# A gated mix of two spectral filters on one core: l = 512 from the gate's products, and the first inverse step in column tiles

## Chip, core and metric

The kernel runs on one core of a Trainium2 chip. The metric is the device time of one execution in microseconds (us). Before the change the median of three runs is 132.49 us (131.15, 132.49 and 135.37). One further execution was recorded by the profiler. It took 130.99 us, and its instructions span 129.2 us.

## The reference

One input of 2048 x 1024 goes through two spectral filters; a gate made from each row of the input mixes the two results.

```python
def _A_ref(x, w_r, w_i):          # _B_ref is the same with B's weights
    B, S, D = x.shape
    X = jnp.fft.rfft2(x.astype(jnp.float32), axes=(-2, -1))
    X = X * (w_r + 1j * w_i)
    return jnp.fft.irfft2(X, s=(S, D), axes=(-2, -1)).astype(jnp.bfloat16)

x = A_x                            # (1, 2048, 1024), bf16
g = _sigmoid((x * gate_w).sum(-1, keepdims=True))
a = _A_ref(x, A_w_r, A_w_i)
b = _B_ref(x, B_w_r, B_w_i)
return g * a + (1 - g) * b
```

The transform has 513 columns, l = 0 to 512. Column l = 512 doesn't fit the 512 wide tiles and is carried separately.

## The kernel before

**Stages.** Everything is a matrix product with constant matrices. Row s of the input is split as 16 p + n2, with p on the 128 partitions.

1. *S1* (`xrows`, `stage_s1`): for each of 16 n2, VectorE folds the columns by symmetry and TensorE transforms over p. The result Z is kept in `R3`.
2. *gate rows* (`gate_row`, c = 0 to 3): products of Z with the folded gate weights, in column tiles of TensorE: 4 tiles of 32 output partitions work side by side, in two waves of 512 columns. An eviction (`zrow`) and four small products (`zg`) follow.
3. *D* and *S2*, for 16 groups kg: `stage_d` makes the transform along the columns (8 matmuls of 256 columns), evicted to Q; `stage_s2` finishes the transform along the rows (4 matmuls of 512 columns), evicted to X. `stage_d` also has two matmuls of one column each (into `xd`), which make column l = 512.
4. *Products* (`prod(b, m)`): for branch b (0 is A, 1 is B) and pair m of groups, 2 multiplications (2048 elements a partition) and 2 additions (1024) on VectorE. Three pairs differ. Those in `SPLIT` have the two multiplications alone, and the one in `LATE` has four of half the size; for these three the additions are left to TensorE, which accumulates four products where it otherwise takes two.
5. *First inverse step, I1* (`stage_i1`): for each kg of a pair, 4 matmuls of 128 x 128 weights and 512 columns (8 for `SPLIT` and `LATE`), then an eviction V into a tile `ub` of the ring (at most 6 at once).
6. *Turn*: from `ub` two DMAs, one for each half h of the rows, move 128 KB each from 64 partitions, 2 apart, to 8 partitions, 4 apart. They land in `U`: `R1` for A, and `R3` for B once Z has been read. There are 64 turns, all on SP's queue.
7. *Column 512* (`x512`, `p512`, `v512`): the same steps in small. It ends in two tiny writes a branch (`U5`).
8. *Second inverse step, Sj* (`inverse`): for each of 16 n2, 8 products with A's U and 8 with B's, with the gate mixed into the matrices `RA` and `RB`. Then eviction T, the inverse along the columns (`Dinv`), eviction, and four additions that unfold the result (`h0`, `h1`, `y0`, `y1`), and the output DMA. Half h = 0 of U serves n2 = 0 to 7 and h = 1 the others. An Sj of n2 = 0 to 7 needs the h = 0 turns of *all* groups of its branch.

**What sets the order.** A list scheduler (`Plan.run`) goes through all operations; `TABLE` gives each its engine (p TensorE, a ScalarE, v VectorE, s SP) and a place in that engine's queue. An operation starts in the plan when its inputs are there and its tiles are free. The engines then run the planned order in strict sequence with semaphores. SP's queue is strictly in order too: a turn that waits for its V holds up all later ones. The evictions are shared between ScalarE and VectorE as the table says.

**Lines.** L502 is every matmul, L505 every two-input VectorE operation, L529 and L530 the evictions on ScalarE and VectorE, L535 every DMA, L895 the gate's sigmoids. `RING` holds product tiles, `ub`, Q and `gz`; `SK` holds the matrices of S2 and I1; `MS` small constants; `PS` is PSUM.

Of the kernel before, what the change touches and what calls it, by code (L numbers as in the profile page):

```python
# [9 lines left out]
ALU = mybir.AluOpType  # L10
AP = bass.AP
BF = dt.bfloat16

NS = 513
# [4 lines left out]
s1374 s1438 s1501 s1564 s1627 s1690 s1754 s1817 s1880 s1944 v90 p160 v508 v522 v890 a638 p1558 a1678 v583 v441 v475  # L19
v549 p684 a830 p597 a738 v638 v698 p859 a1013 p772 a921 v829 v769 p946 a1104 p1034 a1196 v966 v1026 p1208 v1348  # L20
p1121 a1287 v1157 v1097 p1582 a1690 p1296 a1404 v1288 v1228 p1383 a1495 p1470 a1587 v1556 v1462 p1810 a1930 p1669
a1781 v1616 v1683 v1650 v1522 v1731 v1804 p1909 v1974 p1953 a2021 p1756 a1873 p1998 p2064 v2149 p2278 p2010 v2088
p2392 p2130 a2390 p2495 v2528 p2686 a2799 s1999 s2062 s2188 s2252 s2378 s2441 s2505 s2568 s2631 s2694 s2758 s2821
s2884 s2947 s3011 s3074 p2174 a2299 p2408 a2531 p2299 a2439 p2600 a2707 v2918 v3145 v3031 v3205 p3322 a3441 s3550
s3611 p3588 a3715 s3825 s3885 p2507 v2621 p2783 a2890 p2689 v2804 p2962 a3075 v3265 v3492 v3379 v3552 p4120 a4264
s4434 s4374 p3674 a3807 s3946 s4006 p2869 a2983 p3142 a3258 p3049 a3166 p3408 a3532 v3726 v3900 v3960 v4187 p4379
a4539 s4738 s4678 p4292 a4447 s4557 s4617 p3228 a3349 p3940 a4081 p3494 a3624 p3760 a3898 v4427 v4715 v4313 v4540
p4828 a4945 s5055 s5115 p5000 a5128 s5238 s5298 p3847 a3990 p4206 a4356 p4026 a4173 p4558 a4666 v4788 v5015 v4902
v5076 p5353 a5494 s5664 s5604 p5180 a5311 s5481 s5421 p4465 v4601 p4741 a4854 p4648 a4762 p5439 a5586 v5831 v6058
v5944 v6118 p6252 a6417 s6526 s6587 p6338 a6508 s6647 s6708 p5087 a5220 p5619 a5769 p5525 a5677 p5798 a5952 v6178  # L30
v6429 v6303 v6489 p6759 a6883 s7053 s6992 p6618 a6741 s6851 s6911 p5705 a5860 p6526 a6650 p5885 a6051 p6163 a6325
v6957 v7144 p7282 a7476 s7658 s7597 p7455 a7649 s7819 s7758 a6043 p6151 v6292 v7131 v6416 v7665 v8662 v8367 v8076
v8705 v8202 v4074 v4247 v3613 v3840 p5266 a5403 s5542 s6115 p4914 a5037 s5176 s6054 v7258 v7431 v7552 v7789 p7887
a7994 s8257 s8136 p7973 a8086 s8317 s8196 v5249 v5423 v5136 v5363 p6937 a7066 s7234 s7537 p6851 a6974 s7113 s7174
v5597 v5770 v5483 v5710 p6064 a6234 s6433 s6373 p5978 a6142 s6312 s6252 v6610 v6837 v6723 v6897 p7023 a7157 s7355
s7295 p7110 a7249 s7476 s7416 v7963 v8212 v8089 v8273 p8491 a8598 s8710 s8892 p8405 v8514 s8650 s8831 v7675 v7849
p8059 a8253 s8378 s8438 p8232 a8480 s8589 s8771 v7071 v7492 v7371 v6550 p7196 p7757 p7628 a7827 a7778 s7954 s7894
p7671 p7800 p7844 a7876 a7925 s8015 s8075 p8685 a8728 p8763 v8808 v8816 p8728 v8772 p8807 v9006 v9231 s5999 p6492
a6600 v8380 v8447 p6424 a6833 v8333 v8413 p6469 a8430 v8672 v8719 p6447 a8380 v8480 v8628 p8876 p9096 p9156 a9202
p9664 a9776 p8921 p9006 p9090 v9117 p9352 v9461 v9885 v9946 v10019 v10140 s10214 p8831 p9045 a9111 p9220 a9329 p9484  # L40
p9574 v9709 p9841 a9949 v10080 v10200 v10374 v10549 s10622 p9308 p9529 v9595 p10062 a10223 p10189 p10329 a10394
p10506 a10614 v10850 v10729 v11024 v11145 s11218 p9796 p9973 a10040 p10373 a10486 p9928 p10018 a10132 p10241 v10435
v10669 v10609 v10790 v11084 s11158 p9751 p10150 p10234 v10260 p10772 v10910 p10461 p10593 p10677 a10705 p10904
a11017 v11205 v11265 v11446 v11569 s11643 p10682 p10859 a10925 p11079 a11200 p10632 p10727 a10797 p10992 a11108
v11325 v11386 v11509 v11630 s11703 p9440 p9619 a9685 p11345 a11505 p11166 p11256 a11322 p11433 a11596 v11766 v11705
v11859 v11953 s12027 p11211 p11301 a11413 p11565 a11688 v11920 v11826 v12014 v12068 s12115 p11520 p11652 a11779
p11888 a11953 v12047 v12121 p11932 a12002 v12101 v12142 v12176 s12223 v12209 s12258"""
QD = False
SPLIT = ((0, 7), (1, 6))
LATE = ((1, 7),)  # L50
# [7 lines left out]
def bf16_bits(a):  # L58
    a = np.ascontiguousarray(np.asarray(a, dtype=np.float32))
    u = a.view(np.uint32).astype(np.uint64)  # L60
    return ((u + 0x7FFF + ((u >> 16) & 1)) >> 16).astype(np.uint16)


def make_consts():
# [20 lines left out]
    turned = np.array([8 * (4 * a + b) + e for a in range(4) for e in range(8) for b in range(4)])  # L85
# [62 lines left out]
    KI = KI.reshape(2, 2, 128, 2, 2, 8, 8).transpose(2, 0, 1, 3, 6, 5, 4).reshape(128, 1024)  # L148
# [4 lines left out]
    M = np.zeros((128, 410))  # L153
    for h in range(2):
        M[:, 408 + h] = (-1.0) ** (np.arange(128) + 1)
    M[turned, 280 + np.arange(128)] = 1.0
    M[:, :16] = gs.reshape(128, 1)
    M[::32, 16] = 1.0
    for kg in range(16):
        M[kg, 152 + 32 * (kg // 4) + kg % 4] = 1.0  # L160
# [292 lines left out]
def bass_gated_mix__spectral_gfnet__spectral_gfnet__prompt_kernel(  # L453
# [11 lines left out]
    def ap(t, off, dims, p0=0, np_=128):  # L465
# [10 lines left out]
    MS = sb("MS", 410)  # L476
# [70 lines left out]
    def cload(eng, t, off, key, a, b, keys, **kw):  # L547
# [3 lines left out]
    P.add("zero8", {"dve": (0.1, 0.2)}, lambda e: [lambda e: e.memset(ap(G8, 0, [[1, 8]]), 0.0)], [], ["G8"])  # L551
    P.add("table", {"act": (1.4, 1.5)}, lambda e: [lambda e: e.activation(ap(ZG, 0, [[1, 8]]), ap(G8, 0, [[1, 8]]), ACT.Sigmoid)],
          ["G8"], ["ZG"])
# [11 lines left out]
    cload("sp", MS, 0, "MS", 0, 410, ["MS"])  # L565
# [54 lines left out]
    ev("g8", 8, lambda: (ap(G8, 0, [[1, 8]]), psl(gp, 0, [[1, 8]])), [(gp,)], ["G8"], only="act")  # L620
# [4 lines left out]
    def gate_row(c):  # L625
# [3 lines left out]
        def fns():  # L629
            return [mm(psl(t, 0, [[1, 512]], 32 * j, 32), ap(G8, 2 * j + r, [[0, 32]]),  # L630
                       ap(R3, (2 * j + r) * 128 + c * 32, [[1024, 16], [1, 32]]), r == 0, r == 1)
                    for r in range(2) for j in range(4)]
        pe("gate", [512] * 2, fns, ["G8"] + [("Z", 4 * c + i, j) for i in range(4) for j in range(2)], [(t,)], alloc=[t])
        ev("zrow", 512, lambda: (rg(gz, 0, [[8, 16], [128, 4], [1, 8]]), psl(t, 0, [[32, 16], [8, 4], [1, 8]])),
# [3 lines left out]
           [(gz, 0, 1), "MS"], [(gzps,)], alloc=[gzps] if c == 0 else [])  # L638

# [69 lines left out]
    x5, xd = Tile("p1", 1), Tile("p1", 1)  # L709

    def stage_d(kg):
# [14 lines left out]
        pe("D", [256] * 8 + [1] * 2, fns, allz(kg // 8) + ["DM", "MS"], [(t,), (xd,)], alloc=[t] + ([xd] if kg == 0 else []))  # L726
# [23 lines left out]
    def prod(b, m):  # L750
# [6 lines left out]
        if (b, m) in LATE:  # L757
            p = PT[b, m] = [[Tile("tl", 2) for _ in range(2)] for _ in range(2)]
            for kg in range(2 * m, 2 * m + 2):
                P.key = ("PA", "PB")[b], m  # L760
                for c, t in enumerate(p[kg % 2]):
                    P.add("mul", vt(1024), lambda e, t=t, c=c, kg=kg: [tt(
                        rg(t, 0, [[512, 2], [1, 512]]), ap(R4, kg * 1024, [[512, 2], [1, 512]]),
                        ap(T, kg * NS + c * NW, [[NW - 2 * c * NW, 2], [1, 512]]), ALU.mult)],
                        [("X", kg)] + wkeys(b, (kg,)), [(t, 0, 2)], alloc=[t])
            return
# [15 lines left out]
    def stage_i1(b, m):  # L782
# [3 lines left out]
        wide = isinstance(p, list)  # L786
        terms = [(768, 0, 0), (1792, 0, 512), (1024, 1, 0), (1024, 1, 512)] if wide else [(768, 0, 0), (1024, 0, 512)]

        def data(r, i):
            return rg(p[terms[i][1]] if wide else p, r * 1024 + terms[i][2], [[1, 512]])  # L790

        def matrix(r, i, o, w):
            return ap(SK, terms[i][0] + (512 if r == m == 0 else 0) + o, [[1, w]])

        def turns(u, kg, parts=1):
            for h in range(2):
                def turn(h=h):
# [222 lines left out]
```

## Time and profile before

| | us |
|---|---|
| runs, lowest / median / highest | 131.15 / 132.49 / 135.37 |
| profiled execution: time, span | 130.99, 129.2 |
| busy: PE, VectorE (DVE), ScalarE (ACT) | 114.4, 106.5, 99.7 |
| TensorE clock granted, mean | 0.992 |

How to read the views: a table of windows gives, for each stretch of the span, each engine's busy time with the number of instructions, the granted clock, the share of time for which the core's 16 DMA engines were busy, and what they moved. The chain of waits follows the last instruction back to what released it. A timeline lists runs of like instructions, with start and length. Matmul ends are modelled: a 512 column matmul is shown as 379 ns, while in an unbroken stream the next one starts 0.216 us after it, so throughput is read from starts.

From the span's start: S1 and the gate rows run to about 23 us, D, S2, products, I1 and turns from there to about 94 us, and the second inverse step with its output to the end.

### The profile page before, as it was taken

The numbers are of one execution on the slowest core, as the hardware profiler recorded it, in microseconds if no ns is written. First come the engines' busy times: TensorE is split into PE (matmuls) and PEld (weight loads), VectorE is DVE, ScalarE is ACT, GpSimd is POOL, SyncE is SP. The second block draws the span as 40 slices with busy tenths as digits, with TensorE's granted clock in tenths as the row PEclk, the third lists the DMA queues.
The fourth block names the chain that finished last, engine by engine and source line by source line (L and its number), as shares of the span: only waits on it lengthen the run. The fifth ranks groups of instructions, "written<-read, shape, count | busy, mean of one in ns | idle before, by whom it ended". The sixth has DMA issues, their size and how long they took to land.

```text
span 129.2 us, 2533 instructions
## 1 busy us (share of the span) xinstructions
PE 114.4 (89%) x993; PEld 75.9 (59%) x999; DVE 106.5 (82%) x163; ACT 99.7 (77%) x115; POOL 0.2 (0%) x4
## 2 busy tenths in 40 slices
PE   6779999999999999999998899985769999999530
PEld 2358867676656454556453343431659999999520
DVE  1578996249999999999999989799143899999992
ACT  4359899577999999999997938786144587999940
POOL 0000000000000000000000000000000000000000
PEclk9999999999999999999999999999999999999996
DMA  4999999999998434344655445555520004408466
GB/s 108 359 374 424 414 393 360 391 382 385 380 373 319 173 105 148 101 154 153 207 174 159 160 147 180 174 191 193 195 100 0 5 0 162 167 0 325 171 247 238
DMA packets 14046, 28.08 MB, mean 217 GB/s; under 512 B 1489, under 2 KB 6097, under 8 KB 14034
## 3 DMA queue, kind: packets, MB, share of 16 engines
q1 hardware_dynamic: 14032, 27.91, 60.0%
q8 instruction: 8, 0.13, 0.4%
q14 instruction: 4, 0.03, 0.1%
q10 hardware_dynamic: 2, 0.00, 0.0%
HBM read 15.33 MB, written 4.19 MB: 151 GB/s over the span
## 4 chain that ended last, share of the span: by engine, by line
PE 53%; DMA 19%; ACT 12%; DVE 9%; issue 3%; SPq 2%; DVEq 0%; ACTq 0%
PE PS L502 53%; DMA R<-RING 14%; ACT R L529 7%; DVE RING L505 6%; ACT RING L529 5%; DMA R<-in_A_x_dram 4%; DVE R L505 3%; SPq L535 2%; ACT RING L895 0%; DVEq L267 0%; DVE R L530 0%; DVE P L505 0%; ACTq L253 0%; DVE X L530 0%; DVEq L253 0%
## 5 line engine op out<-in xcount | busy, mean ns | idle before, releaser
L529 ACT ACTIVATE R<-PS 128x1024 bf16<-128x1024 f32 (+1 forms) x56 | 54.8, 1033 | 15.6 <-PE PS L502 15.5
L505 DVE TENSOR_TENSOR RING<-R 128x2048 bf16<-128x2048 bf16 (+2 forms) x54 | 48.8, 942 | 6.5 <-DMA R<-in_A_x_dram 4.4
L502 PE MATMUL PS<-RING,SK 128*128 128x512 bf16 x210 | 49.6, 379 | 1.6 <-ACT RING L529 0.7
L529 ACT ACTIVATE RING<-PS 128x1024 bf16<-128x1024 f32 (+1 forms) x48 | 45.3, 1028 | 7.3 <-DMA R<-RING 4.4
L502 PEld LDWEIGHTS PS<-RING,SK 128*128 128x128 bf16 x216 | 19.8, 98 | 25.4 <-ACT RING L529 3.7
L502 PE MATMUL PS<-DM,R 128*128 128x256 bf16 (+1 forms) x256 | 26.7, 245 | 0.7 <-DMA R<-RING 0.4
L502 PEld LDWEIGHTS PS<-DM,R 128*128 128x128 bf16 x256 | 18.6, 97 | 5.8 <-ACT R L529 1.0
L505 DVE TENSOR_TENSOR R<-R 128x1024 bf16<-128x1024 bf16 (+2 forms) x38 | 20.3, 599 | 0.7 <-ACT R L529 0.5
L505 DVE TENSOR_TENSOR RING<-RING 128x1024 bf16<-128x1024 bf16 x28 | 18.2, 683 | 0.1
L502 PE MATMUL PS<-DI,R 128*128 128x256 bf16 x128 | 16.1, 273 | 2.4 <-ACT R L529 2.4
L530 DVE CAST R<-PS 128x1024 bf16<-128x1024 f32 (+1 forms) x13 | 11.5, 903 | 6.9 <-PE PS L502 6.8
L502 PE MATMUL PS<-R,RING 128*128 128x256 bf16 (+1 forms) x128 | 13.8, 266 | 1.8 <-DVE RING L505 1.8
L502 PEld LDWEIGHTS PS<-DI,R 128*128 128x128 bf16 x128 | 11.8, 98 | 3.9 <-ACT R L529 2.7
L502 PEld LDWEIGHTS PS<-R,RING 128*128 128x128 bf16 x128 | 11.6, 98 | 4.2 <-DVE RING L505 2.6
L502 PE MATMUL PS<-RING,R 128*128 128x128 bf16 x128 | 8.8, 219 | 0.0
L502 PEld LDWEIGHTS PS<-RING,R 128*128 128x128 bf16 x128 | 7.8, 98 | 0.2
L530 DVE CAST RING<-PS 128x1024 bf16<-128x1024 f32 (+1 forms) x6 | 6.2, 1040 | 1.4 <-PE PS L502 1.4
L502 PE MATMUL PS<-MS,R 128*128 128x1 bf16 (+1 forms) x40 | 5.2, 165 | 0.0
L502 PE MATMUL PS<-RING 128*128 128x512 bf16 x10 | 3.8, 558 | 1.2 <-DVE RING L597 1.2
L502 PEld LDWEIGHTS PS<-MS,R 128*128 128x128 bf16 (+1 forms) x40 | 3.4, 96 | 0.4 <-issue 0.2
L502 PEld LDWEIGHTS PS<-RING 128*128 128x128 bf16 x10 | 1.3, 137 | 3.2 <-issue 1.9
L895 ACT ACTIVATE RING<-PS 128x512 bf16<-128x512 f32 x4 | 2.7, 702 | 0.3 <-DMA R<-RING 0.3
(35 smaller groups left out, 20.5 us busy)
## 6 DMA issues: line engine op xcount, KB each, us to landing
R<-RING SPq DMA_DIRECT2D x64, 128.0 KB
R<-in_A_x_dram SPq DMA_DIRECT2D x8, 512.0 KB, 7.9
out_dram<-R SPq DMA_DIRECT2D x7, 512.0 KB, 3.1
R<-in_A_w_r_dram SPq DMA_DIRECT2D x7, 256.5 KB, 9.3
R<-in_A_w_i_dram SPq DMA_DIRECT2D x7, 256.5 KB, 9.3
R<-in_B_w_i_dram SPq DMA_DIRECT2D x7, 256.5 KB, 8.4
R<-in_B_w_r_dram SPq DMA_DIRECT2D x7, 256.5 KB, 8.2
R<-c_F SPq DMA_DIRECT2D x2, 256.0 KB, 5.3
```

Source lines behind the costliest of these rows:

```text
L502: return lambda e: e.matmul(o, l, r, start=start, stop=stop, skip_group_check=True)
L505: return lambda e: e.tensor_tensor(out=o, in0=a, in1=b, op=op)
L529: return [lambda e: e.activation(o, i, ACT.Copy)]
L530: return [lambda e: e.tensor_copy(o, i)]
L535: lambda e: [lambda q, d=d, s=s: q.dma_start(d, s) for d, s in pairs()],
L895: P.add("sig", {"act": (0.5, 0.7)}, lambda e: [lambda e: e.activation(rg(gr, 0, [[1, 512]]), psl(t, 0, [[1, 512]]), ACT.Sigmoid)], [(t,)], ...
```

## The change

**Column 512.** The gate's matrix has 32 columns, of which the program used copies of one. They now hold the gate weights and, apart from them, alternating signs, so that the same gate products also give column 512 on another partition. `stage_d` loses its two one-column matmuls in each of the 16 groups, and `x512` loses an eviction. In their place each gate row gets a DMA (`q5`) of 1 KB in runs of 32 bytes, on SP's queue. The tile `gz` stays occupied until that DMA has read it.

**First inverse step.** I1 of a pair m is organised by the half h instead of by the group. For each h, the two groups of the pair are computed side by side in two column tiles of 64 output partitions: 8 matmuls of 64 columns of weights and 512 columns of data, in 4 waves of two (16 in 8 waves for a `SPLIT` pair). V then holds one half of both groups, and one DMA of 256 KB turns it: from 128 partitions to 16 partitions, 8 apart. There are 32 turns in place of 64. The constants are permuted to match (`row_of`, `turned`, `KI`, `MS`).

**Products.** `LATE` goes, and `SPLIT` keeps one pair, (1, 7); pairs (0, 7) and (1, 6) get their additions on VectorE.

**Plan.** I1 is its own kind for the planner, which charges TensorE 0.11 us for a change of kind. The tile limits change, and the whole table is new: 523 entries in place of 556 (p 153 for 157, v 165 for 163, a 112 for 115, s 93 for 121). In the order of the new table the 32 I1 groups stand in 13 unbroken runs on TensorE; the gate row c = 2 and the `zg` products move from before the first D to the midst of the D stage, and the mixing of `RA` and `RB` stands behind all products.

```diff
-SPLIT = ((0, 7), (1, 6))
-LATE = ((1, 7),)
+SPLIT = ((1, 7),)
...
+def row_of(kg):
+
+    m, r = divmod(kg, 2)
+    return m + 64 * r, 8
...
-    KI = KI.reshape(2, 2, 128, 2, 2, 8, 8).transpose(2, 0, 1, 3, 6, 5, 4).reshape(128, 1024)
+    KI = KI.reshape(2, 2, 128, 2, 2, 8, 8).transpose(2, 0, 1, 3, 4, 6, 5).reshape(128, 1024)
...
-    M = np.zeros((128, 410))
+    M = np.zeros((128, 448))
     for h in range(2):
-        M[:, 408 + h] = (-1.0) ** (np.arange(128) + 1)
...
+        M[:, 428 + 2 * h] = (-1.0) ** (np.arange(128) + 1)
...
-              "t": ("ring", 3), "tn": ("ring", 2), "tl": ("ring", 4), "pp": ("ring", 4), "g": ("ring", 2), "gz": ("ring", 2), "RA": ("ring", 1), "ub": ("ring", 6), "w": ("ring", 1), "T": ("t", 5),
-              "o": ("late", 2), "h": ("late", 2), "y": ("late", 3), "yl": ("late", 2)})
+              "t": ("ring", 2), "tn": ("ring", 4), "pp": ("ring", 3), "g": ("ring", 2), "gz": ("ring", 2), "RA": ("ring", 1), "ub": ("ring", 5), "w": ("ring", 1), "T": ("t", 4),
+              "o": ("late", 3), "h": ("late", 2), "y": ("late", 3), "yl": ("late", 2)})
...
-        n.kind = {"gate": 2}.get(name, 0)
+        n.kind = {"I1": 1, "gate": 2}.get(name, 0)
...
-            return [mm(psl(t, 0, [[1, 512]], 32 * j, 32), ap(G8, 2 * j + r, [[0, 32]]),
-                       ap(R3, (2 * j + r) * 128 + c * 32, [[1024, 16], [1, 32]]), r == 0, r == 1)
-                    for r in range(2) for j in range(4)]
+            return [mm(psl(t, 0, [[1, 512]], 32 * j, 32), ap(MS, 408 + qq[r], [[1, 32]]),
+                       ap(R3, qq[r] * 128 + c * 32, [[1024, 16], [1, 32]]), r == 0, r == 1)
+                    for r in range(2) for j, qq in enumerate(((0, 1), (2, 3), (4, 6), (5, 7)))]
...
-        ev("zrow", 512, lambda: (rg(gz, 0, [[8, 16], [128, 4], [1, 8]]), psl(t, 0, [[32, 16], [8, 4], [1, 8]])),
+        ev("zrow", 512, lambda: (rg(gz, 0, [[1, 16], [128, 4], [16, 8]]), psl(t, 0, [[32, 16], [8, 4], [1, 8]])),
...
+        dma("q5", "sp", lambda: [(ap(Q5, 0, [[1, 16]], 32 * c, 32), rg(gz, 0, [[16, 32], [1, 16]], 80, 1))],
+            0.06, 400, [(gz, 0, 1)], [("Q5", c)], n=1.15)
...
-                    if g == 2:
-                        f.append(mm(psl(xd, kg, [[1, 1]]), z, ap(MS, 408 + h, [[1, 1]]), h == 0, h == 1))
...
-        for r in range(2):
-            kg = 2 * m + r
-            P.key = ("IA", "IB")[b], kg
-            t, u = Tile("ps", 2), Tile("ub", 2)
-
-            def fns(r=r, t=t):
-                return [mm(psl(t, o * 512, [[1, 512]]), matrix(r, i, o * 128, 128), data(r, i), i == 0, i == len(terms) - 1)
-                        for o in range(2) for i in range(len(terms))]
...
-            turns(u, kg)
...
+        p0, step = row_of(2 * m)
+        for h in range(2):
+            P.key = ("IA", "IB")[b], 2 * m + h
+            t, u = Tile("ps", 2), Tile("ub", 2)
...
+                    for i, (k, j, v) in enumerate(terms):
+                        for r in range(2):
+                            z = k + (512 if r == m == 0 else 0) + o * 128 + h * 64
+                            src = p[j] if isinstance(p, list) else p
+                            f.append(mm(psl(t, o * 512, [[1, 512]], 64 * r, 64), ap(SK, z, [[1, 64]]),
+                                        rg(src, r * 1024 + v, [[1, 512]]), i == 0, i == len(terms) - 1))
...
+            dma("turn", "sp", lambda u=u, h=h: [(AP(T, p0 * pt + h * 8192, [[step * pt, 16], [1024, 8], [1, 1024]]), rg(u, 0, [[1, 1024]]))],
+                0.262, 205, [(u, 0, 2)], [("U", b, m, h)], n=1.15, after=allz(h) if b else [("x", i) for i in range(16)])
...
-        ev("q5", 16, lambda: (ap(Q5, 0, [[1, 16]]), psl(xd, 0, [[1, 16]])), [(xd,)], ["Q5"])
```

More of the change, by code (lines that the diff above doesn't have):

```diff
@@ L23 @@
[L23 to L27, printed above, removed]
@@ L84, in make_consts @@
     R[0, 1] = ((-1.0) ** np.arange(128))[None, :] / 2048
-    turned = np.array([8 * (4 * a + b) + e for a in range(4) for e in range(8) for b in range(4)])
+    turned = np.zeros(128, int)
+    for kg in range(16):
+        p, step = row_of(kg)
+        turned[p + step * np.arange(8)] = 8 * kg + np.arange(8)
     C["RM"] = R.reshape(128, 2048)[turned]
@@ L756, in prod @@
         r = [("X", 2 * m), ("X", 2 * m + 1)] + wkeys(b, (2 * m, 2 * m + 1))
[L757 to L766, printed above, removed]
         if (b, m) in SPLIT:
@@ L785, in stage_i1 @@
         pt = pit[id(T)]
[L786 to L797, printed above, removed]
-                    return [(AP(T, (32 * (kg // 4) + kg % 4) * pt + h * 8192, [[4 * pt, 8], [1024, 8], [1, 1024]]),
-                             AP(RING, h * pit[id(RING)] + u.at * CELL, [[2 * pit[id(RING)], 64], [1, 1024]]))]
-                dma("turn", "sp", turn, 0.131, 200, [(u, i * 2 // parts, (i + 1) * 2 // parts) for i in range(parts)], [("U", b, kg, h)], n=1.1,
-                    after=allz(h) if b else [("x", i) for i in range(16)])
@@ L803, in stage_i1 @@
-        if (b, m) in LATE:
-            z = 512 if m == 0 else 0
-            for r in range(2):
-                kg = 2 * m + r
-                P.key = ("IA", "IB")[b], kg
-                u, ts = Tile("ub", 2), [Tile("p1", 1) for _ in range(2)]
-                for c, os in ((0, (0, 1)), (1, (0,)), (1, (1,))):
-                    def part(c=c, os=os, r=r, ts=ts):
-                        return [mm(psl(ts[o], 0, [[1, 512]]), ap(SK, k + (z if r == 0 else 0) + o * 128, [[1, 128]]), rg(p[r][c], v, [[1, 512]]),
-                                   c == 0 and v == 0, c == 1 and v == 512)
-                                for o in os for k, v in (((1024, 0), (1024, 512)) if c else ((768, 0), (1792, 512)))]
-                    pe("I1", [512] * 2 * len(os), part, [(p[r][c], 0, 2), "SK"], [(ts[o],) for o in os], alloc=ts)
-                for o in range(2):
-                    ev("V", 512, lambda t=ts[o], u=u, o=o: (rg(u, o * 512, [[1, 512]]), psl(t, 0, [[1, 512]])), [(ts[o],)], [(u, o, o + 1)], alloc=[u])
-                turns(u, kg, 2)
-            return
@@ L838, in fns @@
                     for c, k in ((0, 2), (1, 0)) for a, n in ((1, 15), (0, 1))]
-        pe("x5", [16] * 4, fns, ["Q5", "SK"], [(x5,)])
+        pe("x5", [16] * 4, fns, [("Q5", c) for c in range(4)] + ["SK"], [(x5,)])
         ev("x512", 32, lambda: (ap(X5, 0, [[1, 32]]), psl(x5, 0, [[1, 32]])), [(x5,)], ["X5"])
@@ L871, in v512 @@
             ev("U5", 8, lambda h=h: (ap(UR[b], 512 + h * 8192, [[1024, 8]]), psl(t2, h * 8, [[1, 8]])), [(t2,)], [("U5", b, h)], only="dve",
-               after=[("U", b, kg, h) for kg in range(16)])
+               after=[("U", b, m, h) for m in range(8)])
     for kg in range(16):
@@ L938, in inverse @@
                 g = ("RB", n2 // 4) if b else (RA, n2 // 4, n2 // 4 + 1)
-                u = [("U", b, kg, n2 // 8) for kg in range(16)]
+                u = [("U", b, m, n2 // 8) for m in range(8)]
                 if not b:
```

91 lines of the change are left out of this document (51 added, 40 removed).

## The prediction

> **What bounds the kernel now.** I first read a table of windows: who is busy in which stage.
>
> ```profile
> 30.00:40.00 10.00, 9.95 (x72) 6.29 (x72) 10.00 (x12) 9.99 (x12) 0.00 (x0) 1.00 1.05 378
> 60.00:70.00 10.00, 9.53 (x63) 4.68 (x64) 10.00 (x15) 10.00 (x13) 0.00 (x0) 1.00 0.54 176
> 70.00:80.00 10.00, 9.48 (x44) 3.77 (x42) 9.22 (x14) 6.83 (x9) 0.00 (x0) 1.00 0.50 162
> 80.00:88.00 8.00, 7.58 (x36) 3.27 (x35) 7.07 (x14) 6.30 (x10) 0.00 (x0) 1.00 0.52 182
> 88.00:94.00 6.00, 3.52 (x53) 2.46 (x52) 2.99 (x10) 1.97 (x3) 0.00 (x0) 1.00 0.53 194
> 97.00:117.00 20.00, 20.00 (x273) 18.89 (x272) 17.44 (x24) 15.37 (x17) 0.00 (x0) 1.00 0.16 62
> ```
>
> Columns: window, length, PE, weight loads, VectorE, ScalarE, POOL, clock, DMA share, GB/s. Until 70 us PE, VectorE and ScalarE are full at once; from 70 on VectorE and ScalarE wait, and the turns are the only DMA. From 88 to 94 nobody is full. After 97 PE is full again, in a stage that the change hardly touches. So the place to look is 70 to 96 us. The chain of waits says what ends last there:
>
> ```profile
> 83.86 1.03 ACT RING L529
> ...
> 85.94 3.75 DMA R<-RING
> ...
> 89.77 1.02 ACT RING L529
> ...
> 90.81 3.05 DMA R<-RING
> ...
> 93.91 0.58 PE PS L502 x7
> ...
> 96.50 20.96 PE PS L502 x280
> ```
>
> An eviction V waits for a ring tile that an earlier turn still reads; the last V ends at 90.79, its turn lands at 93.86, and the Sj products with B's U begin at 93.91. To the end of the span it is 129.2 - 93.91 = 35.3 us. The DMA queue's own timeline:
>
> ```profile
> 61.42 31.96 SPq L535 DMA_DIRECT2D R<-RING  x42
> ```
>
> 42 of 64 turns are issued here, 0.76 us apart on average. At 182 to 194 GB/s, 131 KB take 0.70 us: SP and the DMA engines are both close to full. Last, VectorE, which makes the products:
>
> ```profile
> 30.29 2.35 DVE L505 TENSOR_TENSOR RING<-R 128x2048 bf16<-128x2048 bf16 x2
> 32.56 1.28 DVE L505 TENSOR_TENSOR RING<-RING 128x1024 bf16<-128x1024 bf16 x2
> 33.77 2.36 DVE L505 TENSOR_TENSOR RING<-R 128x2048 bf16<-128x2048 bf16 x2
> ...
> 82.54 1.23 DVE L505 TENSOR_TENSOR RING<-R 128x2048 bf16<-128x2048 bf16 x1 [0.93 <-PE PS L502]
> ...
> 85.02 1.29 DVE L505 TENSOR_TENSOR RING<-RING 128x1024 bf16<-128x1024 bf16 x2
> ```
>
> A pair costs 33.77 - 30.29 = 3.48 us: 2.28 for the multiplications, 2 x 0.60 for the additions. From 30.29 to 86.31 VectorE stalls only about 1.7 us (1.1 for PE, 0.6 for a turn). So the last product is set by VectorE's work, and what follows by the turns.
>
> **The change part by part.** *PE.* Two pairs lose 8 matmuls of 512 columns: 16 x 0.216 = 3.45 us. The 32 one-column matmuls, shown at 166 ns each, cost what the next start waits: one at 23.36, the next matmul at 23.39, so 0.03 x 32 = 0.9 us. Against that come the column tiles. The trace has them in the gate rows:
>
> ```profile
> 21.35 1.05 PE L502 MATMUL PS<-R,G 128*32 128x512 bf16 x16
> ```
>
> Sixteen matmuls in four waves: the last ends 0.38 after its start, so four waves start within 0.67 us, 0.22 apart, the pace of single untiled matmuls. Two groups in 4 waves per half then cost what 4 matmuls a group cost: nothing. A change of mode costs: a gate row at 18.85 has streamed by 18.85 + 2 x 0.22 = 19.29, and the next ordinary matmul starts at 19.40 (0.1); on the way in, 0.07 from the zg products (four from 21.18, about 0.03 apart) to 21.35. So 0.17 for each of 13 runs: 2.2 us. Gate row and zg that move into the stage add about 1. PE: -3.45 - 0.9 + 2.2 + 1 = -1.1 us; it is not what ends last.
>
> *VectorE.* Before: 13 pairs x 3.48 + 2 x 2.28 + the LATE pair, 4 x 0.60 = 52.2 us. After: 15 x 3.48 + 2.28 = 54.5: **+2.3 us**, on the path, with nothing to hide it up to 70 us. Its cover would be the stalls: of 1.7 us, those for PE (1.1) go if PE runs ahead with its saved work; I take -1.1, ends -1.7 (all gone) and +1.7 (doubled, as the ring limits are tighter: 5 ub tiles for 6).
>
> *Start.* A gate row (0.43) and four zg groups (0.1 each) no longer precede D, and the first D groups lose 0.06 each: the first product can start 0 to 1.1 us earlier; I take 0.7, since evictions before it set its start too.
>
> Last addition: 86.31 + 2.3 - 1.1 - 0.7 = **86.8**.
>
> *From there to U.* I1 needs both groups' products, as it does now, since each VectorE operation covers both. I1 of the last pair's h = 0: 0.1 for the mode, 4 x 0.22 and 0.2 to drain, 1.2; V 1.0 (row at 89.77): 89.0. Before, 4.5 us lay between the last addition (86.31) and the last V (90.79), because V waited for turns and both groups' I1 were needed; now the h = 1 group serves only the later n2, and its turn is hidden by the first eight Sj. ScalarE's sigmoids and VectorE's RA and RB (8 x 0.34 = 2.7 us) stand behind the last product; they lie beside V and the turn.
>
> *The turn.* 256 KB in one DMA. SP's work falls from 64 issues to 32 plus four q5 (0.65 us each; q5 waits for its gate eviction, with the turns of A queued behind it, in a stretch where the engines are full and the turns are not urgent). The rate isn't in the trace for this shape. Lower end: all 16 engines at today's pace, 0.70 us for 256 KB. Upper end: worse than two old turns, twice 1.40 = 2.8. I take 1.40, no change of rate, since both forms write rows of 2 KB into few partitions. Latency: 3.05 in the last link of the chain, 3.6 to 4.4 in the queued ones; 2.6 to 4.4, taken 3.1. So Sj with B starts at 89.0 + 3.1 = **92.1** in place of 93.9.
>
> The row for the rate is the share 0.50 to 0.53, at which the turns alone saturate, beside 1.05 at 378 GB/s for loads: a turn uses half the engines. [...]
>
> *Sum.* 92.1 + 35.3 = 127.4 us of span. The profiled execution had 1.8 us around its span (130.99 - 129.2), so 129.2 us beside 130.99: -1.8 us, or -1.4%. That execution is the quiet end of the runs (131.15, median 132.49). A median lies between 0 and 1.5 above it; I add 0.6: **129.8 us**.
>
> **Rivals.**
> *A, the turns become twice as fast.* For it: only half of the engines work now. [...] Stalls go (-1.7), the start is 1.1 earlier, the latency 2.6: last addition 85.8, V 88.0, Sj 90.6: span 125.9, time 127.7, by scatter up to 128.5.
> *B, slower: the turn of 256 KB costs more than two old ones.* The place is the last third: in the new table's order 14 of 32 turns stand behind those of pair (1, 3), and so do the products of some six pairs, 6 x 3.48 = 21 us, 1.5 us a turn. From that interval on, less what is queued already, the queue holds up V through the five ub tiles, then the last I1. At 1.6 us it is 14 x 0.2 = 2.8 us over the 1.4 of the sum, 129.8 + 2.8 = 132.6, about no change; at 1.8, 135.4; at 2.0, 138.2. [...] Against it: loads show that 16 engines at once lose nothing (378 GB/s).
> *C, the weight loads of column tiles stay uncovered.* Then each of 15 x 8 + 16 = 136 waves costs about 0.095 more (a load's duration), 12.9 us, less PE's slack of some 4: 138 us or more. The gate rows speak against it: 0.22 a wave, loads included. [...]
> *D, nothing gained.* VectorE keeps its stalls and starts no earlier: 86.31 + 2.3 + 2.2 + 3.1 = 93.9, as before: 131 to 132.5.
>
> **How the numbers follow.** Forecast 0.50, A 0.13, B 0.17, C 0.03, D 0.17. The forecast's own range is 128 to 131.5. The range of all cases reaches from A (127.0, a little under its 127.7 for what the ends of the latency leave open) into B at 1.7 us (129.8 + 14 x 0.3 = 134.0); outside are C, B's worse half. 2% of the measured time (2.6 us) is about what a measurement of this kernel tells from no change. Faster by more: all of A and four tenths of the forecast (129.8 is exactly 2% under 132.49 and 0.9% under 130.99), 0.33. Slower by more: C and most of B, 0.17. Within: 0.50.
>
> **What would show it.** VectorE's pairs 3.48 apart, 30 additions of 1024 among them; I1 groups as 128*64 matmuls two at a time, waves 0.22 apart; 0.1 us at the mode changes. DMA share in 70 to 90 us: 0.5 with 190 GB/s means still eight engines; near 1.0 with about 190 GB/s, sixteen that share something; above 250 GB/s, A. The start of Sj with B (the DM,R matmuls of 128 columns): 92.1; later than 94 is B or D. Wrong it would be, too, if the second inverse step were no longer 35.3 us, as its pools change (T 4 for 5, o 3 for 2).

## The result, and the profile after

The changed kernel takes 132.52 us (median of 20 runs, 131.67 to 135.81), the kernel before, run beside it, 131.69 (20 runs). The ratio is 1.006, 95% interval 1.003 to 1.009. Some executions run over 1.5% longer than the fastest of the same kernel; medians here take in all executions, ratios and intervals leave those out. The forecast was 129.8 us, 1 to 2% less than before; the change makes the kernel 0.6% slower. The profiled execution took 132.08 us, its span is 130.3 us against 129.2.

The two windows of the kernel before that matter now, columns as in the prediction:

```profile
40.00:50.00 10.00, 9.95 (x68) 5.56 (x67) 10.00 (x13) 9.78 (x12) 0.00 (x0) 1.00 0.50 172
50.00:60.00 10.00, 9.95 (x64) 5.72 (x64) 10.00 (x13) 10.00 (x12) 0.00 (x0) 1.00 0.41 134
```

The windows of the changed kernel:

```profile
40.00:50.00 10.00, 8.31 (x69) 4.09 (x68) 8.61 (x10) 9.24 (x9) 0.00 (x0) 1.00 0.86 172
50.00:60.00 10.00, 9.00 (x85) 4.70 (x83) 8.81 (x14) 10.00 (x12) 0.00 (x0) 1.00 0.37 93
...
70.00:80.00 10.00, 9.51 (x84) 4.38 (x82) 10.00 (x11) 9.28 (x12) 0.00 (x0) 1.00 1.01 243
80.00:88.00 8.00, 7.00 (x64) 3.31 (x60) 8.00 (x10) 5.72 (x7) 0.00 (x0) 1.00 1.06 203
88.00:94.00 6.00, 3.81 (x46) 2.10 (x44) 2.69 (x9) 4.47 (x7) 0.00 (x0) 1.00 0.98 194
```

Two things are new. Between 40 and 60 us TensorE and VectorE are no longer full: VectorE has 17.42 of 20 us, where before it had all 20. That is not where the prediction looked. And from 70 to 94 the DMA share has doubled to about 1.0 at almost the old rate in the last two windows (203 and 194 GB/s, where it was 182 and 194): all sixteen engines work, at half their pace. From 72 to 88 us the 2 KB packets of the turns take 169 ns, sixteen at a time, where they took 84 ns, eight at a time (medians).

What VectorE waited for, from its timeline (in the changed kernel L510 is every matmul, L513 every two-input VectorE operation, L537 and L538 are the evictions on ScalarE and VectorE):

```profile
29.94 2.36 DVE L513 TENSOR_TENSOR RING<-R 128x2048 bf16<-128x2048 bf16 x2
...
33.47 2.37 DVE L513 TENSOR_TENSOR RING<-R 128x2048 bf16<-128x2048 bf16 x2
...
50.37 2.37 DVE L513 TENSOR_TENSOR RING<-R 128x2048 bf16<-128x2048 bf16 x2 [1.76 <-ACT R L537]
...
54.73 0.18 DVE L513 TENSOR_TENSOR ZG<-PS,MS 128x16 bf16<-128x16 f32 x1 [0.79 <-PE PS L510]
...
88.28 1.29 DVE L513 TENSOR_TENSOR RING<-RING 128x1024 bf16<-128x1024 bf16 x2
```

It waits for an eviction on ScalarE (X, L537), and later for TensorE. The last addition ends at 89.57 (86.31 before). Why ScalarE was late stands in the groups of instructions of 20 to 56 us, kept apart by shape (busy time, mean ns of one, idle time before):

```profile
L537 ACT ACTIVATE RING<-PS 128x512 bf16<-128x512 f32 x3 | 7.2, 2409 | 0.0
...
L538 DVE CAST RING<-PS 128x512 bf16<-128x512 f32 x1 | 2.4, 2392 | 0.2 <-PE PS L510 0.2
```

These are the four `zrow` evictions of the gate rows: 2.4 us each. Before, the same 512 elements a partition took 0.60 us on ScalarE and 0.68 on VectorE (the kernel before, 17 to 56 us):

```profile
L530 DVE CAST RING<-PS 128x512 bf16<-128x512 f32 x2 | 1.3, 681 | 0.0
...
L529 ACT ACTIVATE RING<-PS 128x512 bf16<-128x512 f32 x2 | 1.2, 598 | 0.0
```

The last two of the three on ScalarE start at 46.22 and 50.21, where ScalarE is full. Last, the chain of waits at the end of the products:

```profile
86.14 1.07 PE PS L510 x8
...
87.24 1.03 ACT RING L537
...
88.29 5.37 DMA R<-RING
...
93.75 0.19 DVE R L538
93.94 0.30 DVE DM L513
94.24 0.68 DVE RING L513 x2
...
94.97 1.98 PE PS L510 x32
```

A turn of branch A (5.37 us from issue to landing) releases `U5` on VectorE; RA and RB are queued behind that, and Sj with A's U begins at 94.97, with B's at 96.32.

The time can be balanced by four marks, read from the VectorE and TensorE timelines. The later columns are experiments, described below.

| us from the span's start | before | forecast | after | e1_again | e5_early_q5 | e8_u5_behind_mixing |
|---|---|---|---|---|---|---|
| first product starts | 30.29 | 29.6 | 29.94 | 28.59 | 28.81 | 28.72 |
| last addition ends | 86.31 | 86.8 | 89.57 | 86.56 | 85.45 | 85.36 |
| Sj with B starts | 93.91 | 92.1 | 96.32 | 93.40 | 92.19 | 91.92 |
| from there to the end | 35.3 | 35.3 | 34.0 | 34.0 | 34.0 | 34.0 |
| span | 129.2 | 127.4 | 130.3 | 127.4 | 126.2 | 125.9 |

Against the forecast the changed kernel loses 0.35 us up to the first product, 2.4 from there to the last addition and 1.45 from there to Sj, and gains 1.3 in the second inverse step: 2.9 us in all.

### The profile page after: what moved, and what is told of

Its sections match the earlier page's. It is cut to its first block, busy times and chain, and to the rows that moved or that the text cites. A ratio compares the mean times of both kernels' runs of the same rounds, so it can differ in the third digit from the quotient of the medians.

```text
span 130.3 us, 2685 instructions
## 1 busy us (share of the span) xinstructions
PE 112.8 (87%) x1087; PEld 74.8 (57%) x1087; DVE 111.4 (85%) x165; ACT 104.5 (80%) x112; POOL 0.2 (0%) x4
## 4 chain that ended last, share of the span: by engine, by line
DVE 32%; PE 30%; ACT 18%; DMA 9%; issue 8%; SPq 1%; DVEq 0%; ACTq 0%
PE PS L510 30%; DVE RING L513 16%; DVE R L513 12%; ACT RING L537 11%; ACT R L537 6%; DMA R<-in_A_x_dram 4%; DMA R<-RING 4%; DVE R L538 3%; SPq L543 1%; DVE R L612 0%; DVE P L513 0%; DVEq L275 0%; DVE DM L513 0%; ACT X L537 0%; DVEq L261 0%
## 5 line engine op out<-in xcount | busy, mean ns | idle before, releaser
L537 ACT ACTIVATE R<-PS 128x1024 bf16<-128x1024 f32 (+1 forms) x53 | 51.7, 1043 | 12.6 <-PE PS L510 12.5
L537 ACT ACTIVATE RING<-PS 128x1024 bf16<-128x1024 f32 (+1 forms) x49 | 52.1, 1187 | 6.3 <-PE PS L510 5.9
L513 DVE TENSOR_TENSOR RING<-R 128x2048 bf16<-128x2048 bf16 (+2 forms) x52 | 48.1, 976 | 6.3 <-DMA R<-in_A_x_dram 4.4
L510 PE MATMUL PS<-RING,SK 128*64 128x512 bf16 (+1 forms) x336 | 47.0, 381 | 3.4 <-DVE RING L513 3.1
L510 PEld LDWEIGHTS PS<-RING,SK 128*64 128x64 bf16 (+1 forms) x336 | 19.6, 107 | 26.4 <-DVE RING L513 5.0
L510 PE MATMUL PS<-DM,R 128*128 128x256 bf16 (+1 forms) x256 | 24.8, 246 | 0.8 <-ACT RING L537 0.8
L510 PEld LDWEIGHTS PS<-DM,R 128*128 128x128 bf16 x256 | 19.9, 98 | 4.9 <-ACT RING L537 1.6
L513 DVE TENSOR_TENSOR R<-R 128x1024 bf16<-128x1024 bf16 (+2 forms) x38 | 20.8, 602 | 0.3
L513 DVE TENSOR_TENSOR RING<-RING 128x1024 bf16<-128x1024 bf16 x32 | 20.9, 686 | 0.1
L538 DVE CAST R<-PS 128x1024 bf16<-128x1024 f32 (+1 forms) x16 | 15.3, 963 | 5.3 <-PE PS L510 4.2
L510 PE MATMUL PS<-DI,R 128*128 128x256 bf16 x128 | 15.5, 273 | 1.4 <-ACT R L537 1.4
L510 PE MATMUL PS<-R,RING 128*128 128x256 bf16 (+1 forms) x128 | 13.8, 266 | 2.2 <-DVE RING L513 2.2
L510 PEld LDWEIGHTS PS<-R,RING 128*128 128x128 bf16 x128 | 11.5, 98 | 4.6 <-DVE RING L513 3.4
L510 PEld LDWEIGHTS PS<-DI,R 128*128 128x128 bf16 x128 | 11.9, 98 | 3.2 <-ACT R L537 1.7
L510 PE MATMUL PS<-RING,R 128*128 128x128 bf16 x128 | 8.8, 219 | 1.6 <-DVE RING L513 1.6
L510 PEld LDWEIGHTS PS<-RING,R 128*128 128x128 bf16 x128 | 7.6, 98 | 2.3 <-DVE RING L513 2.1
L538 DVE CAST RING<-PS 128x1024 bf16<-128x1024 f32 (+1 forms) x3 | 4.8, 1613 | 0.5 <-PE PS L510 0.5
L510 PE MATMUL PS<-RING 128*128 128x512 bf16 x10 | 4.2, 598 | 1.2 <-DVE RING L605 1.2
L510 PEld LDWEIGHTS PS<-RING 128*128 128x128 bf16 x10 | 1.3, 142 | 3.4 <-issue 2.2
L510 PE MATMUL PS<-R,MS 128*32 128x512 bf16 x32 | 2.1, 382 | 1.3 <-ACT RING L537 1.3
L513 DVE TENSOR_TENSOR RING<-DM,RING 128x512 bf16<-128x512 bf16 x4 | 1.6, 422 | 0.9 <-ACT RING L873 0.9
```

The costliest lines, as they stand in the source:

```text
L510: return lambda e: e.matmul(o, l, r, start=start, stop=stop, skip_group_check=True)
L513: return lambda e: e.tensor_tensor(out=o, in0=a, in1=b, op=op)
L537: return [lambda e: e.activation(o, i, ACT.Copy)]
L538: return [lambda e: e.tensor_copy(o, i)]
```

## The experiments

**The eviction.** The diff also turned the write pattern of `zrow` round. Before, the inner run was 8 neighbouring bf16; now each element lies 16 elements, 32 bytes, from the last. The first experiment gives the changed kernel a walk through the same elements, to the same places, in another order:

```diff
-(rg(gz, 0, [[1, 16], [128, 4], [16, 8]]), psl(t, 0, [[32, 16], [8, 4], [1, 8]]))
+(rg(gz, 0, [[128, 4], [16, 8], [1, 16]]), psl(t, 0, [[8, 4], [1, 8], [32, 16]]))
```

> The changed kernel with the same values in the same places, but the gate row's eviction goes through them in another order: it writes runs of 16 neighbours and reads PSUM with a step of 32 instead of the reverse. Theory (the eviction's 2-byte writes, 32 bytes apart, cost it 2.4 us instead of 0.6, and the two that lie at 46 to 53 us hold up ScalarE, TensorE and VectorE there): each eviction back to 0.6 to 0.7 us, VectorE's stalls between 47 and 55 us (1.8 and 0.8) gone, last addition 2 to 3 us earlier, 2 to 3 us faster than the changed kernel, that is 0.98 to 0.99 of the kernel before. Rival 1 (the cost is in reading PSUM or in the number of dimensions): still about 2.4 us each, no change in time. Rival 2 (the late turns alone set the end, the stalls only shift waiting): evictions short, but less than 0.7 us gained.

129.75 us beside 131.69 before, ratio 0.986 (0.978 to 0.993). The same kernel once more, for its trace:

> e1_row_writes again, for a profile on the same chip as the three others: ratio 0.983 to 0.989; q5 of gate rows 0 and 1 issued near 35 us and landed near 47, ScalarE and VectorE waiting for it.

130.16 us beside 132.28, ratio 0.982 (0.973 to 0.990), just under the expected 0.983 to 0.989. The evictions are back at the old price; the same group of instructions in e1_again:

```profile
L537 ACT ACTIVATE RING<-PS 128x512 bf16<-128x512 f32 x3 | 1.8, 604 | 1.2 <-DMA Q<-RING 1.2
```

The counter-test puts the scattered write, and nothing else of the change, into the kernel before (the constants that read `gz` are permuted to match):

```diff
-(rg(gz, 0, [[8, 16], [128, 4], [1, 8]]), psl(t, 0, [[32, 16], [8, 4], [1, 8]]))
+(rg(gz, 0, [[1, 16], [128, 4], [16, 8]]), psl(t, 0, [[32, 16], [8, 4], [1, 8]]))
```

> The kernel before with one thing of the change: the gate row's eviction writes its values 32 bytes apart, and the two small constants that follow are permuted to match. Theory (2.4 us an eviction wherever it stands; in the kernel before all four stand ahead of the D stage, where ScalarE and VectorE have idle time): four evictions of about 2.4 us, two on each engine, 0.5 to 2.5 us slower than before. Rival (the length comes from what else ran at that time in the changed kernel): 0.6 to 0.7 us each and no change in time.

135.11 us, ratio 1.029 (1.022 to 1.037), more than the 0.5 to 2.5 us that were expected. The idle time ahead of D didn't take the longer evictions up: the chain of waits runs through all four of them, and the first product starts at 33.69 in place of 30.29. The eviction on VectorE, as the trace lists it (shortest, median, longest ns):

```profile
L530 DVE CAST RING<-PS x2: 2343/2430/2518, 22.3 to 24.3; 128x512 bf16<-128x512 f32 x2
```

So the pattern alone costs 2.9% in the kernel before and about 2% in the changed one. It is the step of the inner run in SBUF that costs: e2 changes that side alone, and the PSUM side reads 32 columns apart in e1 and is none the slower for it. On ScalarE the eviction took 0.60 us in runs of 8 neighbours (before) and of 16 (e1), and 2.34 us (e2) to 2.45 with every element 32 bytes from the last: four times as long. What in the write makes that price, no run shows.

**The hold on `gz`.** In e1_again the chain of waits between 25 and 60 us goes through `q5`:

```profile
34.98 11.01 DMA Q<-RING
...
46.08 0.10 ACT RING L537
...
46.57 1.03 ACT R L537
```

SP issues the q5 of rows 0 and 1 behind B's weight loads; 1 KB needs 11 us to land, both `gz` tiles stay occupied, and ScalarE stands still for 1.2 us. The next experiment, on top of e1, changes two entries of the table (written here with the names of their operations), so that these two stand among B's loads; the order of TensorE, ScalarE and VectorE is the same.

```diff
-gate 0, q5: s3137    gate 1, q5: s3200
+gate 0, q5: s2188    gate 1, q5: s2189
```

> The changed kernel with zrow written row by row (as in e1_row_writes) and, besides, the q5 of gate rows 0 and 1 placed on SP's queue ahead of B's weight loads instead of behind them. In e1_row_writes these two were issued at 35.2 and 35.9 us and landed at 47.2 and 47.4, and ScalarE (2.4 us) and VectorE (1.5) then stood waiting for them, because both gz tiles were held. Theory: the second cause of the lost time is that hold; q5 lands before 38 us, the waits for 'DMA Q<-RING' between 44 and 50 us are gone, and the time falls by another 1 to 3 us, ratio to before 0.962 to 0.980. Rival: the engines catch the stall up later, where VectorE and ScalarE wait for the turns anyway (70 to 94 us): ratio as in e1_row_writes, 0.983 to 0.989.

128.65 us beside 132.28, ratio 0.975 (0.967 to 0.984). The q5 land at 32.9 and 33.7, and the windows of e5_early_q5 are full again between 40 and 60 us:

```profile
40.00:50.00 10.00, 9.88 (x91) 5.24 (x90) 10.00 (x12) 9.25 (x12) 0.00 (x0) 1.00 0.93 190
50.00:60.00 10.00, 10.00 (x88) 5.33 (x88) 10.00 (x17) 10.00 (x12) 0.00 (x0) 1.00 0.51 136
```

Sj with B begins 1.2 us earlier than in e1_again. The medians, measured side by side, differ by 1.5 us, but the two intervals overlap; what shows the gain is the trace. The same kernel once more:

> e5_early_q5 again, on the same chip as e7_step_seven_first: ratio to before 0.967 to 0.983, span near 126.2 us, Sj with B from 92.2 us.

128.60 us beside 131.18, ratio 0.981 (0.977 to 0.986), within the expectation. The span of its profile is 127.8, not 126.2: that execution was granted a clock of 0.75 between 88 and 94 us, and Sj with B began at 93.36 there.

Does the hold cost anything in the change as it was made, with the slow eviction?

> The changed kernel with zrow still written 32 bytes apart, and only q5 of rows 0 and 1 ahead of B's weight loads. If the write pattern and the hold each cost on their own (theory), this lies between the changed kernel (1.006) and e5_early_q5: zrow still 2.4 us each, ratio 0.985 to 0.998. If the scattered write is the whole cause and the hold costs nothing (rival), 1.003 to 1.009 as the changed kernel.

132.02 us beside 132.28, ratio 1.000 (0.991 to 1.008): the interval reaches into both expectations and decides nothing. The trace of the changed kernel speaks for the rival: its q5 landed at 46.14 and 46.40, while ScalarE was busy with other evictions until 46.17 and started the third `zrow` at 46.22. The hold lay hidden behind the slow evictions and came out when they were mended.

**The turns, measured by themselves.** A kernel that only moves 2 MB in each of six shapes, from SBUF to SBUF, one shape after the other. For the first two shapes its destinations are, with 8192 elements a partition in D:

```python
AP(D, m * 8192, [[8 * 8192, 16], [1024, 8], [1, 1024]])
AP(D, (32 * (kg // 4) + kg % 4) * 8192, [[4 * 8192, 8], [1024, 8], [1, 1024]])
```

> Not the filter: only SBUF to SBUF transfers of 2 MB each in six shapes, one after the other, with nothing else running, and an output that means nothing. (a) 128 partitions to 16, 8 apart, 256 KB each; (b) 64 partitions, 2 apart, to 8, 4 apart, 128 KB each; (c) to 16 neighbours; (d) to 16, 7 apart; (e) 128 to 128, row to row; (f) to 16, 4 apart. Theory (two engines share one way into the destination partitions): (a) about 205 GB/s at a share of 1.0, (b) about 195 at 0.5, (c) half of (a), (d) well above (a), (e) near 400, (f) like (a). Rival (the limit is on the side of the reads, or the length of packets): (a), (c), (d), (f) all about 205, (e) near 400 or 205. Rival (each engine is slower alone because 16 run at once): (e) also 205.

Its rate by slices of the span (GB/s):

```profile
GB/s 38 76 246 199 216 201 56 72 176 176 184 197 113 126 118 118 119 117 118 119 81 0 277 281 279 80 36 384 378 119 235 201 216 201 69 344 458 351 451 229
```

In order, between the dips: the new turn, 128 partitions to 16 that lie 8 apart, 1.25 us for 256 KB (some 209 GB/s); the old turn, 64 to 8 that lie 4 apart, 176 to 197 GB/s, some 0.7 us for 128 KB (in the kernel before, SP issues two of them 0.64 us apart at the closest); to 16 neighbours, 2.2 us (119); to 16 that lie 7 apart, 1.02 (257 to 281); row to row over all 128, 0.69 (380, with that distance of 0.64 us between two issues close to it); to 16 that lie 4 apart, 1.30 (200). The last pieces are the stores. Twice as many engines, each at half the pace (packets of 169 ns for 84 in the two kernels), give the new turn about the old rate. Both rivals are out: neighbours and 7 apart differ from 8 apart, and row to row reaches 380 GB/s. The theory's order came out: about half the rate of the new turn to neighbours (119 GB/s beside 209), more to 7 apart (257 to 281), like it to 4 apart (200). What it is that the engines share on the way into those partitions, no run shows.

**Do the turns set the end?** Going to partitions 7 apart needs another permutation of the constants, and one pair of groups has to go to 16 neighbours, the slowest shape. This was tried three times, on top of e5. First with pair m = 7 to neighbours:

```diff
-    return m + 64 * r, 8
+    return (112 + 8 * r, 1) if m == 7 else (m + 56 * r, 7)
```

> e5_early_q5 with the turns of 14 of 16 groups going to partitions 7 apart instead of 8 (the pair m = 7 to 16 neighbours), constants permuted to match; column 512's turn takes 16 small products for 8. By itself a turn to partitions 7 apart took 1.02 us and one to 8 apart 1.25, one to neighbours 2.2. Theory: between 70 and 94 us the queue of turns sets the last eviction V, so 28 x 0.25 - 4 x 0.95 = 3 us less in the queue, of which what lies in the saturated stretch (about 14 turns) counts: Sj with B starts 1 to 3 us earlier than in e5_early_q5 and the time is 1 to 3 us less. Rival: VectorE's and TensorE's work sets the last V, and the queue only follows: within 0.5 us of e5_early_q5.

136.11 us, ratio 1.028 (1.020 to 1.036): over 7 us slower than e5, where the theory had 1 to 3 faster and the rival no change. It isn't a clean test. The larger constant table shifted the planner's clock, and the order of all engines changed. But the four turns to neighbours stood together in the full stretch, where they landed 2.4 us apart, and Sj with B began at 98.6, in an execution that was granted a clock of 0.50 between 88 and 94 us. With the order of e5 kept, and pair m = 0 to neighbours:

```diff
-    return m + 64 * r, 8
+    return (m - 1 + 56 * r, 7) if m else (112 + 8 * r, 1)
```

> As e6_step_seven, but with the order of every engine exactly that of e5_early_q5 (in e6 the larger constant table shifted the planner's clock and the order changed), and with pair m = 0, whose turns lie before the saturated stretch, as the one that goes to 16 neighbours; all others go to partitions 7 apart. Theory: in the saturated stretch (70 to 91 us) the turns set the pace, at 1.28 us each; in e6 four turns to neighbours in that stretch landed 2.4 us apart and the start of Sj with B came 7 us later. Now they land about 1.05 us apart, TensorE and ScalarE wait less at 78 to 86 us, Sj with B starts 0.8 to 2 us earlier than in e5_early_q5 (92.2), and the time is 0.5 to 2 us lower. Rival: what VectorE and TensorE do sets the last V; the turns only follow: within 0.4 us of e5_early_q5.

130.94 us, ratio 0.996 (0.992 to 1.000), 1.5% slower than e5_again beside it. Pair 0 was the wrong one: its turns stand directly behind B's loads, and the chain of waits of e7 shows what the slower shape made of that:

```profile
37.97 12.94 DMA R<-RING
...
50.99 1.03 ACT RING L537
```

Five `ub` tiles were not enough for turns that land 13 us after their issue (10 in e5, at most 10.7 in the change). VectorE lost its time there: from 40 to 70 us it is busy 26.7 of 30 us (30.0 in e5). Of the 3.3 us, one wait for a turn, up to 49.53, is 1.88; the clock granted from 50 to 60 us was 0.83 in this execution, so the rest may not all be the turns'. Behind that its pairs ran 3.48 us apart up to the last addition, as in e5 to within 0.3 us in all, although the late turns landed 0.7 to 1.1 us apart. Third, with pair m = 3, whose turns I took to lie apart:

```diff
-    return m + 64 * r, 8
+    return (m - (m > 3) + 56 * r, 7) if m != 3 else (112 + 8 * r, 1)
```

> As e7_step_seven_first, but pair m = 3 goes to neighbours, whose four turns lie apart from each other between 53 and 72 us, in e5_early_q5 unqueued or nearly so. In e7 the pair m = 0 stood behind B's loads, its turns landed 12 to 13 us after issue and held ub tiles, and VectorE lost some 3 us between 45 and 60; behind that its pairs ran 3.48 apart to the end, as in e5_early_q5, while turns landed 0.7 to 1.1 apart. So I now expect that VectorE's products set the last addition and the faster turns change nothing before it: last addition at 85.4 +- 0.4 as in e5_early_q5, late turns 0.7 to 1.1 us apart, Sj with A some 0.5 us earlier because A's last turn lands earlier, time 0 to 0.8 us under e5_early_q5 (ratio 0.970 to 0.982). The theory of e6 and e7 (the turns set the pace there) would have the last addition 0.8 us earlier or more and the time 1 us or more lower.

134.03 us, ratio 1.017 (1.009 to 1.025): wrong again, and by the same mechanism. Two of the four turns were issued at 68.59 and 71.34, behind the 512 KB load of the matrices RM at 67.00, and landed 8.6 and 8.5 us later. The chain, and VectorE's timeline, of e9:

```profile
71.34 8.47 DMA R<-RING
```

```profile
79.91 2.37 DVE L513 TENSOR_TENSOR RING<-R 128x2048 bf16<-128x2048 bf16 x2 [4.38 <-DMA R<-RING]
...
89.15 1.28 DVE L513 TENSOR_TENSOR RING<-RING 128x1024 bf16<-128x1024 bf16 x2
```

The 4.4 us that VectorE stood is nearly the whole difference of the spans (131.2 against 126.2). From 79.91 it runs at 3.48 a pair again. So a late turn is on the path as soon as it lands late enough to keep the ring full, and turns faster than about 1.3 us brought nothing before the last addition: at that rate VectorE's products set it. After it they did bring something: in e7 and e9 `U5` has no turn to wait for, and Sj with B begins 6.3 us after the last addition, where e5 needs 6.74. What seven apart would bring with no slow pair was not tried.

**VectorE against TensorE.** On top of e1, a second pair's additions go back to TensorE:

```diff
-SPLIT = ((1, 7),)
+SPLIT = ((0, 6), (1, 7))
```

> As e1_row_writes, and the additions of pair (0, 6) go back to TensorE (that pair takes 16 waves instead of 8 and VectorE loses two additions, 1.2 us). Theory (VectorE's product chain sets the last product): 0.5 to 1.2 us faster than e1_row_writes. Rival (the turns' queue, 1.27 us for each 256 KB from 72 us on, sets the end): within 0.4 us of e1_row_writes. Rival (TensorE has no room for 1.7 us more): 0.5 us or more slower than it.

130.78 us, ratio 0.996 (0.991 to 1.000), about 1% slower than e1, as the last rival had it in size. The last addition ends at 85.96 against 86.56 in e1_again, half of the 1.2 us that VectorE no longer has to do. The other half went into a longer wait for q5 (0.98 us ahead of VectorE's eviction at 46.97, 0.24 in e1_again). And TensorE pays with 8 more waves of 0.216, 1.7 us: it has no idle time left between 80 and 88 us (8.00 busy, 5.44 in e1_again), and Sj with A begins at 91.72 against 92.05. Where the rest of the 1% lies its profile doesn't settle, since the clock fell to 0.84 in its 88 to 94 us.

**The order at the end.** In e5_early_q5 VectorE and TensorE did this:

```profile
89.62 0.20 DVE L538 CAST R<-PS 128x8 bf16<-128x8 f32 x1 [1.05 <-DMA R<-RING]
...
90.84 1.52 PE L510 MATMUL PS<-RING,R 128*128 128x128 bf16 x24 [1.58 <-DVE RING L513]
```

`U5` waits for A's turn, with RB and RA behind it. The last experiment lets `U5` of A come after three of the RB operations, so that it stands behind six of the eight mixing operations; nothing else moves.

```diff
-after=[("U", b, m, h) for m in range(8)]
+after=[("U", b, m, h) for m in range(8)] + ([] if b else [("RB", c) for c in (0, 2, 3)])
```

> e5_early_q5 with one thing moved on VectorE alone: the two U5 writes of branch A stand behind six of the eight RA and RB operations instead of ahead of RB(3). In e5_early_q5 VectorE waited 1.1 us in front of U5, for the last turn of A with h = 0 (issued 84.2, landed 89.5), with RB and RA queued behind, and Sj with A began at 90.8, Sj with B at 92.2. Theory: 0.5 us of the stretch from the last addition to Sj is that order; Sj with A begins at about 90.3, Sj with B at 91.6 to 91.9, the time falls by 0.3 to 0.6 us, too little for the comparison (ratio 0.970 to 0.982). Rival: Sj is held by the last turn of B (landed 91.2) and by the fourth sigmoid, and starts where it did.

```profile
90.31 0.19 DVE L538 CAST R<-PS 128x8 bf16<-128x8 f32 x1
...
90.56 1.51 PE L510 MATMUL PS<-RING,R 128*128 128x128 bf16 x24 [1.40 <-DVE R L538]
...
91.92 1.50 PE L510 MATMUL PS<-DM,R 128*128 128x128 bf16 x24
```

`U5` no longer waits (the turn landed at 89.80), and Sj begins 0.3 us earlier, less than the 0.5 expected for Sj with A. 127.84 us beside 131.79, ratio 0.976 (0.970 to 0.982): the lowest median of the study, 2.4% under the kernel before. The ratio is no better than that of e5 (0.975 and 0.981); the gain over e5 is only in the trace.

## Why the prediction was wrong

**The step that failed** is the one on the gate rows: "Gate row and zg that move into the stage add about 1", with the start "since evictions before it set its start too". It counted TensorE's share of the moved rows, and forgot their evictions. In the diff quoted ahead of the prediction the write of `zrow` goes from runs of 8 to single elements 32 bytes apart; I read it as a relabelling and costed it at nothing. It made four evictions of 0.6 us into four of 2.4, two of them ahead of the first product and two inside the stretch where ScalarE, VectorE and TensorE are all full. Undone (e1), the span is 127.4 us, the forecast's own figure, and the ratio 0.982 to 0.986 where the forecast stood at 0.980. The agreement is partly luck, as the marks show: the hold on `gz` and the way from the last addition to Sj cost more than forecast, the start and the second inverse step less.

**Start.** 0.7 us earlier was forecast, with 1.1 as the end. It is 0.35 with the slow evictions and 1.5 to 1.7 without them.

**VectorE.** The 2.3 us of additional work are right, and so is the pace of 3.48 a pair. Of the stalls, "I take -1.1, ends -1.7 (all gone) and +1.7": in e5 none is left between the first product and the last addition, and the stretch from first product to last addition is 56.64 us against 56.02, which is 2.3 less 1.7. In the change itself the stalls grew instead, and the stretch is 59.63. The tighter ring (5 `ub` tiles) cost VectorE nothing at about 1.3 us a turn. ScalarE waited 1.0 us for a turn ahead of the V at 83.19 in e5, and the turn of that V is the one for which `U5` waits.

**TensorE.** The changes of mode cost what was taken: in e5 the next matmul starts 0.31 us after one of 512 columns where the mode changes, and 0.216 elsewhere, so 0.19 for each of the 13 runs beside 0.17.

**q5** "waits for its gate eviction, with the turns of A queued behind it ... not urgent". The queue was right: between 30 and 70 us no engine waited for a turn. What I left out was the tile that q5 reads. That cost nothing visible in the change and 1.2 us once the evictions were mended.

**From the last addition to Sj.** Taken 5.3 us, measured 6.74 to 6.84 in the change, e1_again and e5, and 6.56 in e8. I1 and V were right: in e5 V ends 2.17 us after the last addition, 2.2 was taken. The last turn of B needed 3.57 us for 3.1. The remaining 1 us is the sentence that RA and RB "lie beside V and the turn": they stood behind `U5`, which waited for A's last turn, 5.3 us under way, where 2.6 to 4.4 had been allowed. Without that wait 0.2 to 0.5 us of it is gone (e8, e7, e9). The rest is the mixing itself, which in e8 starts behind the first sigmoid, at 88.05 (2.7 us after the last addition), and takes 2.2 us up to `U5`, and A's products, 1.36 us, which come ahead of B's.

**The turn.** The share of 1.0 in place of 0.5 says sixteen engines, eight before, and the packets in flight, sixteen and eight at a time, say the same. In the queue a turn of 256 KB takes about 1.3 us where 1.40 was taken: the rate hardly changed, as forecast. The reason beside it, "both forms write rows of 2 KB into few partitions", was the author's estimate, and the number of partitions alone is not it: to 16 of them a turn took 1.02 us at 7 apart, 1.25 at 8 apart and 2.2 to neighbours. Rival A (0.70 us) is out. Rival B's price wasn't reached by the change, but e6, e7 and e9 show its mechanism, with turns of 2.4 us and more. That rival B at 1.6 us a turn gives 132.6 us, all but the measured time, is a coincidence: the turn took 1.3. Rival C is out: the 16 matmuls of a pair's two halves take 1.92 us in e5, 8 waves of 0.216, weight loads included, and the drain; the gate rows had shown the same, with waves 0.22 apart. Rival D came nearest in time (131 to 132.5) for another reason: VectorE didn't keep its stalls but got new ones, 40 to 60 us.

**The second inverse step** was held at 35.3 us; it takes 34.0 in the change, e1_again, e5 and e8, all with the new pools and table. The prediction named this as a way to be wrong. It hid 1.3 us of the loss; which of T, `o` and the new order makes it wasn't tried.

## What to carry to other kernels

Read every access pattern in a diff, not only the operations: here an inner step of 32 bytes in a write made an eviction four times as long (2.4 us for 0.60), and the row to hold it against is the same instruction with the old pattern. A small transfer cost its time in the queue here, not its size (1 KB took 11 us to land behind B's weight loads), and what it holds meanwhile is a tile: look for who needs that tile next. Before speeding a queue up, look whether the engine that feeds it ever waits for it: here a slower turn cost microseconds at once, a faster one gained nothing before the last addition and 0.4 us behind it.

## What the runs showed of the hardware that was not expected

Evictions from PSUM of 512 elements a partition that write bf16 at a step of 32 bytes take 2.4 us on ScalarE and on VectorE alike, 4.7 ns an element, in place of 0.60 and 0.68 to 0.69; reading PSUM 32 columns apart cost nothing (604 ns). A DMA of 1 KB issued behind weight loads landed 10.7 us later in the change, 11.01 in e1_again and 11.97 in e1_row_writes; the quickest of the change's four took 1.7. Two turns of 256 KB to 16 neighbouring partitions, behind a load of 512 KB, landed 8.6 and 8.5 us after issue, and each such turn took 2.2 us alone and 2.4 in a row.
